# Three edits to an eight-batch attention and MLP kernel: where batch 3's loads are queued, how the ninth chunk's attention is multiplied and evicted, and the order of half-size products

## The chip, the cores and the metric

The kernel runs on one core of a Trainium2 chip. The metric is the device time of one execution in microseconds (us). The engines are named as in the profile: PE is TensorE (matmuls; PEld its weight loads), DVE is VectorE, ACT is ScalarE, POOL is GpSimd, SP is SyncE, which here only issues transfers. Each engine works through its own queue in order. Transfers issued by POOL go into queue q0, those issued by SP into q1.

## The reference

```python
def _attn_ref(q, k, v):                      # (8, 8, 576, 64) each
    q_s = softmax(q over the last axis); k_s = softmax(k over axis 2)
    kv = np.einsum('bhsd,bhse->bhde', k_s, v)
    return np.einsum('bhsd,bhde->bhse', q_s, kv)

def _moe_ref(x, g_ln, w_ch1, w_ch2):         # x: (8, 576, 512), heads side by side
    xn = (x - mean) / sqrt(var + 1e-6) * g_ln
    return x + np.maximum(xn @ w_ch1, 0.0) @ w_ch2     # 512 -> 2048 -> 512
```

The softmax lines are shortened here: the reference subtracts the maximum, and divides by the sum plus 1e-9. All is in float32; the kernel multiplies in bf16 and sums in float32.

## The kernel before

**Chunks.** Each of the 8 batches has 576 rows. The first 512 of each make a chunk (chunk c belongs to batch c), kept as 4 tiles t of 128 rows. The 64 rows left over of all batches are put together as a ninth chunk, C9 = 8: its tile t holds batch 2t in partitions 0 to 63 and batch 2t + 1 in partitions 64 to 127. A chunk passes through attention and then through the MLP, and while PE works on the MLP of chunk c, the attention of chunk c + 1 is slipped in between.

**Attention of a chunk.** ACT takes exp of q (`exp_q`, L193) and k (`exp_k`, L174). A DMA transpose turns exp(q) into `eqT` (`eq_T`, L256). PE forms k·v per pair of heads in `pkv` (`kv_mm`, L308), and DVE writes it, normalised, block-diagonally into `kv_sb` (L318). `po_mm` then multiplies: four matmuls of 128 columns for one tile (L342) into one bank `po`; `x_fast` evicts the bank in one DVE pass (L403) that also multiplies by the reciprocal of the softmax sum and gives the row sum, and `xn_out` (L389) centres the row. `square_sum` (ACT, L377) gives the variance. `xn_T` transposes xn by DMA, two tiles at a time, into `xnT`. `sum_x` (L248) forms four half-size sums `tq` of xnT for the MLP, two instructions each, on POOL for chunks under 8 and on DVE for chunk 8.

In chunk C9 two batches lie in one tile, so `po_mm` multiplies all 128 rows with the kv of both batches (L349, 256 columns, two matmuls in a bank) and half of every result is thrown away: for each pair of matmuls DVE takes the half rows that count in two pieces (L358, 64 partitions x 256). That pass gives no row sum, so `x_rest` takes it on ACT (L418, `AF.Copy` with an accumulator) ahead of `square_sum`.

**MLP of a chunk.** Both matmuls are done with seven half-size products in place of eight (Strassen's scheme in Winograd's form): products 1 to 7 of sums of quarters. In the first matmul (`mm1_fast`, L733) the hidden rows are split in four groups g; groups are taken in pairs (0, 1) and (2, 3). A product of one group is four matmuls of 256 columns. Bank `bx` gets products 1, 6, 7 and 4; ACT copies it after product 1 into `bc` (`seed`, L757), product 5 goes to `bb` and is copied by ACT to `s` (`copy_5`, L761), DVE adds after product 6 (`add_5`, L764: bb = bx + s) and after product 7 (`out_22`, L767, writes hT), and ACT's relus (L779) end the banks. DVE relus what `out_22` wrote for two groups in one instruction (L772). The order that `slot` gives for a pair is: 1, 5 of the first group, 1, 5 of the second; 6, 2 of each; 7, 3 of each; 4 of each.

For the second matmul DVE makes four half-size sums s1 to s4 of the hidden rows, `sum_h(g, i)` (L573), for two halves g of the hidden rows and i = 0 to 3 (s1, s2, s3, s4). `mm2_fast` (L589) takes the products in the order 1, 5, 6, 2, 7, 3, 4, 16 matmuls each, into banks ba, bb, bc, be. Product 5 reads s1, 6 reads s2, 7 reads s3, 3 reads s4. ACT copies ba to s2 and s3 (L614), DVE adds (L617) and makes the output `ot` in quarters (L600), and POOL issues the store (L606). Chunk 8 has its own order (`last_products`: 1, 2, 6, 5, 7, 3, 4) and output tile `yl` (L629). Chunk 0 and the first matmul of chunk 1 use plain matmuls (`ph`, L497, L482; `pc`, L542).

**What sets the order.** Everything is written by hand. `run(main, side)` walks the MLP's steps of one chunk, whose weights add up to a position (one matmul of 256 columns is 0.5, of 512 columns 1); each side step has a position and is issued before the first MLP step at or behind it. `attn_fast` gives the positions of an ordinary chunk's attention, `attn_rest` those of C9, `second_side` those of everything that runs beside chunk 1's MLP, and the list in the call of `run` for chunk 0 those beside chunk 0. `at={7: [...]}` in `mm2_fast` runs steps behind the matmul of that number in a product. In each engine's queue this order is fixed.

**Loads.** `load_batch` clears one element on DVE (L1074) and issues q (L118, 1 MB) or k with its rest (L118, L125) on SP. `load_v` issues v on POOL: for batches 1 and 2 as one transfer into `vt`, copied by `cast_v` (L134), for later ones as four column pieces straight into `vm` (L147) and two of the rest `vr` (L150). `vm` and `vr` have two places, by the batch's parity. In `second_side` q of batch 3 is loaded at position 8, k at 31, `eq_T(2)` stands at 14.2, `load_v(3)` at 12, `load_v(4)` at 60.

**Buffers.** `mm_ps` has six PSUM banks, `att_ps` (pkv, po) two. A new tile waits for the last reader of the bank that it is given.

Of the kernel before, what the change touches and what calls it, by code (L numbers as in the profile page):

```python
# [20 lines left out]
def kernel(  # L21
# [214 lines left out]
    def sum_x(c, i):  # L236
# [9 lines left out]
        eng = nc.gpsimd if c < C9 else nc.vector  # L246
# [88 lines left out]
    def po_mm(c, t, i):  # L335


        if c < B:
            if i == 0:
                pool, tag = (mm_ps, "m") if c == 0 and t >= 2 else (att_ps, "a")  # L340
                pobox["p"] = pobox[c, t] = pool.tile([P, DM], FP32, tag=tag, name="po")
            nc.tensor.matmul(  # L342
                pobox["p"][:, i * P : i * P + P], eqTs[c][:, t, i, :], kv_sb[:, c, i, :],
                start=True, stop=True,
            )
        else:
            if i % 2 == 0:
                pobox[i // 2] = att_ps.tile([P, 2, 2, P], FP32, tag="a", name="po")
            nc.tensor.matmul(  # L349
                pobox[i // 2][:, i % 2], eqTs[c][:, t, i, :],  # L350
                kv_sb[:, 2 * t : 2 * t + 2, i, :], start=True, stop=True,
            )
            if i % 2 == 1:
                hs = slice(2 * i - 2, 2 * i + 2)
                x = xs[c][0][:, t].rearrange("p (h d) -> p h d", h=H)
                for half in range(2):
                    ps = slice(64 * half, 64 * half + 64)
                    nc.vector.tensor_mul(  # L358
                        x[ps, hs, :].rearrange("p (j h) d -> p j h d", h=2),
                        pobox[i // 2][ps, :, half].rearrange("p j (h d) -> p j h d", h=2),  # L360
                        eqs[c][2][ps, t, hs].rearrange("p (j h) -> p j h", h=2).to_broadcast([64, 2, 2, D]),
                    )
# [51 lines left out]

    def x_rest(t):

        x, _, _, mv = xs[C9]
        nc.scalar.activation(  # L418
            scrap, x[:, t], AF.Copy, accum_out=mv[:, t, 0:1]
        )  # L420
        square_sum(C9, t)
# [197 lines left out]
    def last_products(product):  # L619
# [28 lines left out]
        def seed_e():  # L648
# [5 lines left out]
            15: [lambda: both("a", 0, 0), lambda: sum_h(1, 2), lambda: sum_h(1, 3)]})  # L654
        product(2, "c", first=True, at={15: [lambda: both("c", 0, 0, True), lambda: store(0, 2, 0)]})
        product(6, "a", at={15: [lambda: copy_u("s2")]})
# [9 lines left out]
    def mm2_fast(c):  # L666
# [34 lines left out]
        def sums(*which):  # L701
            return [lambda g=g, i=i: sum_h(g, i) for g, i in which if g or c == FAST]

        late, wide = c == FAST, ((1, 2), (1, 3))
        product(1, "a", first=True, cut=6, at={
            0: sums((1, 0), (0, 1), (1, 1)) + ([] if late else sums(*wide[:2 if c < B - 1 else 0])),
            15: [seed_c]})
        product(5, "b", first=True, cut=4, at={
            8: sums((0, 2), (1, 2)) if late else sums(*wide[:1]) if c == B - 1 else []})
        product(6, "a", at={  # L710
            8: sums((0, 3), (1, 3)) if late else sums(*wide[1:]) if c == B - 1 else [], 15: [lambda: copy_u("s2")]})
# [24 lines left out]
    def mm1_fast(c):  # L736
# [37 lines left out]
        def out_relu(g, name, odd, half, eng):  # L774
            dst = h_out(g, odd, half)
            if eng is nc.vector:
                nc.vector.tensor_scalar_max(dst, in0=at[g, name], scalar1=0.0)
            else:
                nc.scalar.activation(dst, at[g, name], AF.Relu)  # L779

        def slot(g, n):
            if n == 0:
                if g == 0:
                    steps.append((0, new_h))
                product(1, g, "x", True, [lambda: seed(g)])
                product(5, g, "b", True, [lambda: copy_5(g)])
            elif n == 1:
                product(6, g, "x", False, [lambda: add_5(g)])
                product(2, g, "c", False, [
                    lambda: out_relu(g, "c", 0, 0, nc.scalar)])  # L790
            elif n == 2:
                product(7, g, "x", False, [lambda: out_22(g)])
                product(3, g, "b", False, [lambda: out_relu(g, "b", 0, 1, nc.scalar)])
            else:
                product(4, g, "x", False, [lambda: out_relu(g, "x", 1, 0, nc.scalar)])

        for g0 in (0, 2):
            for n in range(4):
                for g in (g0, g0 + 1):
                    slot(g, n)  # L800
# [62 lines left out]
    def attn_fast(c):  # L863
# [10 lines left out]
        s += spread([lambda i=i: sum_x(c, i) for i in range(4)], 84, 100)  # L874
        return s

    def second_side():
# [5 lines left out]
        s += [(p, lambda w=w: load_batch(3, (w,))) for p, w in ((8, 2), (31, 0))]  # L883
        s += [(9 + 2 * j, lambda j=j: cast_v(2, j)) for j in range(2)]
        s += [(12, lambda: load_v(3)), (60, lambda: load_v(4))]
# [19 lines left out]
    def attn_rest():  # L905

        s = [(2, lambda: recip_q(C9)), (4, lambda: start_x(C9))]
        for t, (p0, p1, p2, p3) in enumerate(
            ((6, 14, 18, 24), (16, 27, 48, 58), (59, 67, 69, 73), (69, 77, 79, 82))
        ):  # L910
            s += spread([lambda t=t, i=i: po_mm(C9, t, i) for i in range(NP)], p0, p1)
            s += [(p2, lambda t=t: x_rest(t)), (p3, lambda t=t: xn_out(C9, t))]
        s += [(68, lambda: xn_T(C9, 0, 2)), (82.5, lambda: xn_T(C9, 2, 2)), (88, lambda: rstd_op(C9))]
# [278 lines left out]
```

## Time and profile before

| | us |
|---|---|
| median of 3 runs | 284.44 (284.18 to 284.64) |
| the profiled execution | 284.36 |
| its span, first to last instruction | 282.6 |
| PE busy in the span | 269.2 |
| DVE busy | 225.2 |
| ACT busy | 185.6 |
| chunks 3, 4, 5, 6, by their first matmul to the next's | 26.77, 26.77, 26.78, 26.76 |

The page gives each engine's busy time, share of the span and number of instructions; then the span in 40 slices with busy tenths and the granted clock of PE. A PE that is busy is not one at its peak: lengths of matmuls overlap, and a dense run is told by the spacing of starts. Matmul records of 256 columns are 273 ns long and 109 ns apart in a dense run. The waits list who waited for whom, with the total, the number of times and the longest. In a timeline a line is a run of equal instructions: start, length of the run, engine, line, operation, output and inputs, sizes, number, and in brackets how long the engine had stood idle and what ended that. "SPq" is a transfer's issue on SP.

### The profile page before, as it was taken

To read this page: it belongs to the slowest core of one execution; us is meant where nothing else is said; L and a number is where in the kernel's file an instruction comes from. 1 tells how busy PE (TensorE), PEld (TensorE's weight loads), DVE (VectorE), ACT (ScalarE), POOL (GpSimd) and SP (SyncE) were. 2 spreads that over 40 slices of the span, in tenths; PEclk is the share of its full clock that TensorE was granted. 3 is DMA by queue.
4 is the path that set the end of the run, shared out by engine and by line. 5 is a ranking of instruction groups with operands and counts; after the bars stand their busy time and mean duration, and the time that the engine had idled before them with its cause. 6 is when DMAs were issued, how large, how long until landed. Compare 5 with 4: busy or idle time off the path is not lost.

```text
span 282.6 us, 6420 instructions
## 1 busy us (share of the span) xinstructions
PE 269.2 (95%) x2477; PEld 227.3 (80%) x2477; DVE 225.2 (80%) x495; ACT 185.6 (66%) x354; POOL 91.3 (32%) x142
## 2 busy tenths in 40 slices
PE   8999999993999999999999999999999989799994
PEld 5888855771598988998899889898989878688883
DVE  4656795955598899699979997999699898886863
ACT  4547881694397778678858876886788488438600
POOL 3832216356009520781096018003600820011000
PEclk9979999998699999999999999999999999999999
DMA  7999999899968999399849986317803430123014
GB/s 187 243 207 211 332 211 324 190 225 181 200 86 231 266 246 137 87 322 177 150 127 342 84 151 187 129 37 150 259 9 63 87 148 3 37 64 124 2 38 111
DMA packets 85409, 44.99 MB, mean 159 GB/s; under 512 B 62145, under 2 KB 82113, under 8 KB 85378
## 3 DMA queue, kind: packets, MB, share of 16 engines
q0 software_dynamic: 35632, 22.29, 44.1%
q1 hardware_dynamic: 49154, 21.77, 33.5%
q10 hardware_dynamic: 592, 0.52, 0.6%
q8 instruction: 19, 0.31, 0.5%
q14 instruction: 12, 0.10, 0.1%
HBM read 36.70 MB, written 9.44 MB: 163 GB/s over the span
## 4 chain that ended last, share of the span: by engine, by line
PE 81%; DVE 10%; DMA 5%; ACT 1%; issue 1%; DVEq 0%; ACTq 0%
PE ba L589 17%; PE bx L733 16%; PE bb L733 8%; PE ph L497 5%; PE pc L542 4%; PE bb L589 4%; PE be L589 4%; PE bc L589 4%; DMA eqT<-eq 4%; PE bc L733 4%; PE warm L850 4%; PE pkv L308 3%; PE po L342 2%; DVE x L358 2%; PE ph L482 2%; DVE hs L573 2%
## 5 line engine op out<-in xcount | busy, mean ns | idle before, releaser
L589 PEld LDWEIGHTS <-hs 128*128 128x128 bf16 x512 | 49.6, 98 | 7.0 <-issue 1.3
L733 PEld LDWEIGHTS <-w_q 128*128 128x128 bf16 x448 | 41.1, 98 | 5.0 <-issue 0.8
L248 POOL TENSOR_TENSOR tq<-xnT 128x256 bf16<-128x256 bf16 x24 | 15.5, 663 | 91.0 <-DMA xnT<-xn 91.0
L589 PEld LDWEIGHTS <-hT 128*128 128x128 bf16 x384 | 37.2, 98 | 4.4
L733 PEld LDWEIGHTS <-w1g 128*128 128x128 bf16 x336 | 31.3, 98 | 5.9 <-issue 2.1
L733 PE MATMUL bx<-tq,w_q 128*128 128x256 bf16 x224 | 35.1, 273 | 0.2 <-DVE bb L764 0.2
L589 PE MATMUL ba<-w_q,hs 128*128 128x256 bf16 x256 | 31.9, 272 | 1.1 <-ACT s L614 1.1
L764 DVE TENSOR_TENSOR bb<-bx,s 128x512 f32<-128x512 f32 x28 | 19.5, 698 | 12.7 <-ACT s L761 6.6
L757 ACT COPY bc<-bx 128x512 f32<-128x512 f32 x28 | 16.5, 589 | 16.8 <-PE bx L733 16.8
L342 PE MATMUL po<-kv_sb,eqT 128*128 128x128 bf16 x128 | 22.1, 224 | 4.8 <-DMA eqT<-eq 4.6
L403 DVE SCALAR_TENSOR_TENSOR x<-po,rq 128x512 bf16<-128x512 f32 x30 | 20.5, 684 | 6.8 <-PE po L342 6.6
L210 DVE TENSOR_REDUCE zq<-eq 128x16 f32<-128x1024 bf16 (+1 forms) x20 | 20.7, 1050 | 4.9 <-ACT eq L201 2.5
L606 POOL DMA_DIRECT2D out_dram<-ot x28 | 15.3, 553 | 25.8 <-DVE ot L600 25.8
L377 ACT ACTIVATE scrap<-x,mv 128x512 bf16<-128x512 bf16 x32 | 23.1, 721 | 0.6 <-DVE x L403 0.2
L779 ACT ACTIVATE hT<-bc 128x512 bf16<-128x512 f32 x28 | 16.7, 597 | 9.0 <-PE bc L733 8.5
L779 ACT ACTIVATE hT<-bb 128x512 bf16<-128x512 f32 x28 | 16.6, 595 | 9.0 <-PE bb L733 9.0
L573 DVE TENSOR_TENSOR hs<-hT 128x1024 bf16<-128x1024 bf16 x32 | 21.8, 685 | 0.4
L308 PE MATMUL pkv<-vm,ek 128*128 128x130 bf16 x112 | 21.3, 220 | 0.0
L147 POOL DMA_DIRECT2D vm<-in_v_dram x20 | 17.7, 904 | 7.6 <-PE pkv L308 7.1
L767 DVE TENSOR_TENSOR hT<-bx,s 128x512 bf16<-128x512 f32 x28 | 18.6, 687 | 0.8 <-PE bx L733 0.4
L342 PEld LDWEIGHTS <-eqT 128*128 128x128 bf16 x128 | 12.1, 101 | 7.4 <-DMA eqT<-eq 5.1
L733 PE MATMUL bb<-xnT,w_q 128*128 128x256 bf16 x112 | 17.8, 273 | 0.0
(146 smaller groups left out, 610.4 us busy)
## 6 DMA issues: line engine op xcount, KB each, us to landing
out_dram<-ot POOLq DMA_DIRECT2D x32, 256.0 KB, 4.3
qt<-in_q_dram SPq DMA_DIRECT2D x5, 1024.0 KB, 8.7
kt<-in_k_dram SPq DMA_DIRECT2D x5, 1024.0 KB, 8.2
vm<-in_v_dram POOLq DMA_DIRECT2D x20, 128.0 KB, 10.3
w_raw<-in_moe_w_ch_dram POOLq DMA_DIRECT2D x4, 512.0 KB, 12.3
w_sb<-in_moe_w_ch_dram POOLq DMA_DIRECT2D x4, 512.0 KB, 17.7
qt<-in_q_dram POOLq DMA_DIRECT2D x2, 1024.0 KB, 15.5
kt<-in_k_dram POOLq DMA_DIRECT2D x2, 1024.0 KB, 13.7
```

The lines of the kernel that those rows point to most:

```text
L147: nc.gpsimd.dma_start(vm[:, b % 2, t, :, 0:D], src[:, t])
L210: nc.vector.reduce_sum(eqs[c][1][:, ts], eqs[c][0][:, ts], axis=AX.X)
L308: nc.tensor.matmul(pkv[:, j % 2, 0:w], lhsT, rhs, start=(t == 0 and j % 2 == 0), stop=(t == last), skip_group_check=True,)
L342: nc.tensor.matmul(pobox["p"][:, i * P : i * P + P], eqTs[c][:, t, i, :], kv_sb[:, c, i, :], start=True, stop=True,)
L377: nc.scalar.activation(scrap, x[:, t], AF.Square, bias=mv[:, t, 0:1], scale=-float(DM), accum_out=mv[:, t, 1:2],)
L403: nc.vector.scalar_tensor_tensor(x[:, t].rearrange("p (h d) -> p h d", h=H), in0=pobox[c, t].rearrange("p (h d) -> p h d", h=H), scalar=1. ...
L573: nc.vector.tensor_tensor(out=dst, in0=x, in1=y, op=op)
L589: nc.tensor.matmul(hbox[bank][:, t], lhsT, rhs, start=first and (own or t == 0) and k == 0, stop=k == KH - 1, skip_group_check=True)
L733: nc.tensor.matmul(dst[:, q], lhsT, rhs, start=first and q == 0 and ko == 0, stop=ko == 1, skip_group_check=True)
L764: nc.vector.tensor_tensor(out=at[g, "b"], in0=at[g, "x"], in1=at[g, "s"], op=ALU.add)
L767: nc.vector.tensor_tensor(out=h_out(g, 1, 1), in0=at[g, "x"], in1=at[g, "s"], op=ALU.add)
L779: nc.scalar.activation(dst, at[g, name], AF.Relu)
```

## The change

1. **Loads.** In `second_side` q of batch 3 goes from position 8 to 14.3, behind `eq_T(2)`. `load_v(3)` leaves position 12 there and goes to position 109 beside chunk 0's MLP. `load_v(4)` goes from 60 to 90; its place in POOL's queue stays the same, since nothing of POOL's lies between.
2. **Ninth chunk.** `po_mm` for C9 uses two half-row matmuls per pair of heads: 64 columns of weights each, the first half into partitions 0 to 63 of the bank, the second into 64 to 127, each with its own batch's kv, 128 columns. All four pairs of heads go into one bank, and `x_fast` and `square_sum` evict it as in any other chunk. `x_rest` is gone. The positions in `attn_rest` are new.
3. **Products.** `mm1_fast` takes each product for both groups of a pair before the next product: 1, 1, 5, 5, 6, 6, 2, 2, 7, 7, 3, 3, 4, 4. The sums `sum_h` are moved: in chunks 2 to 6 sums s1, s2 and s3 of the first half stand at 30, 33 and 41 (before 33, 36, 39 and 42 for all four), s3 of the second half with s1 and s2 at the start of the second matmul, and both halves of s4 behind half of product 6. In chunk 7 s3 and s4 of both halves are moved behind half of products 5 and 6, in chunk 8 behind products 2 and 6.
4. **Sums of xn.** In `attn_fast` the four `sum_x` stand at 84, 88, 92, 101 (before 84, 88, 92, 96); of chunk 7 the second of them is on DVE, at 100.

```diff
@@ sum_x
-        eng = nc.gpsimd if c < C9 else nc.vector
+        eng = nc.vector if c == C9 or (c == C9 - 1 and i == 1) else nc.gpsimd
@@ po_mm
+        if i == 0:
+            pool, tag = (mm_ps, "m") if c == 0 and t >= 2 else (att_ps, "a")
+            pobox["p"] = pobox[c, t] = pool.tile([P, DM], FP32, tag=tag, name="po")
...
         else:
-            if i % 2 == 0:
-                pobox[i // 2] = att_ps.tile([P, 2, 2, P], FP32, tag="a", name="po")
-            nc.tensor.matmul(
-                pobox[i // 2][:, i % 2], eqTs[c][:, t, i, :],
-                kv_sb[:, 2 * t : 2 * t + 2, i, :], start=True, stop=True,
-            )
-            if i % 2 == 1:
...
-                for half in range(2):
-                    ps = slice(64 * half, 64 * half + 64)
-                    nc.vector.tensor_mul(
...
+            for half in range(2):
+                ps = slice(64 * half, 64 * half + 64)
+                nc.tensor.matmul(
+                    pobox["p"][ps, i * P : i * P + P], eqTs[c][:, t, i, ps],
+                    kv_sb[:, 2 * t + half, i, :], start=True, stop=True,
+                )
@@ x_rest
-        nc.scalar.activation(
-            scrap, x[:, t], AF.Copy, accum_out=mv[:, t, 0:1]
-        )
-        square_sum(C9, t)
@@ last_products
-            15: [lambda: both("a", 0, 0), lambda: sum_h(1, 2), lambda: sum_h(1, 3)]})
-        product(2, "c", first=True, at={15: [lambda: both("c", 0, 0, True), lambda: store(0, 2, 0)]})
-        product(6, "a", at={15: [lambda: copy_u("s2")]})
+            15: [lambda: both("a", 0, 0)]})
+        product(2, "c", first=True, at={7: [lambda g=g: sum_h(g, 2) for g in range(2)],
+            15: [lambda: both("c", 0, 0, True), lambda: store(0, 2, 0)]})
+        product(6, "a", at={7: [lambda g=g: sum_h(g, 3) for g in range(2)], 15: [lambda: copy_u("s2")]})
@@ mm2_fast
-            return [lambda g=g, i=i: sum_h(g, i) for g, i in which if g or c == FAST]
+            return [lambda g=g, i=i: sum_h(g, i) for g, i in which if g or c == FAST or i == 3 or c == B - 1 and i > 1]
...
-            0: sums((1, 0), (0, 1), (1, 1)) + ([] if late else sums(*wide[:2 if c < B - 1 else 0])),
+            0: sums((1, 0), (0, 1), (1, 1)) + ([] if late else sums((1, 2))),
...
+            8: sums((0, 3), (1, 3)), 15: [lambda: copy_u("s2")]})
@@ mm1_fast
-        for g0 in (0, 2):
-            for n in range(4):
-                for g in (g0, g0 + 1):
-                    slot(g, n)
+        for g0 in (0, 2):
+            for n, name, first, after in plan:
+                for g in (g0, g0 + 1):
+                    product(n, g, name, first, [lambda g=g, after=after: after(g)])
@@ attn_fast
-        s += spread([lambda i=i: sum_x(c, i) for i in range(4)], 84, 100)
+        s += [((84, 100 if c == C9 - 1 else 88, 92, 101)[i], lambda i=i: sum_x(c, i)) for i in range(4)]
@@ second_side
-        s += [(p, lambda w=w: load_batch(3, (w,))) for p, w in ((8, 2), (31, 0))]
+        s += [(p, lambda w=w: load_batch(3, (w,))) for p, w in ((14.3, 2), (31, 0))]
-        s += [(12, lambda: load_v(3)), (60, lambda: load_v(4))]
+        s += [(90, lambda: load_v(4))]
@@ attn_rest
-            ((6, 14, 18, 24), (16, 27, 48, 58), (59, 67, 69, 73), (69, 77, 79, 82))
+        for t, (p0, p1, p2) in enumerate(((6, 22, 46), (40, 54, 62), (59, 66, 69), (68, 75, 77))):
             s += spread([lambda t=t, i=i: po_mm(C9, t, i) for i in range(NP)], p0, p1)
-            s += [(p2, lambda t=t: x_rest(t)), (p3, lambda t=t: xn_out(C9, t))]
+            s += [(p1, lambda t=t: x_fast(C9, t)), (p2, lambda t=t: square_sum(C9, t))]
@@ beside chunk 0
+            + [(109.0, lambda: load_v(3)), (128.0, lambda: xn_pT(1, 2, nc.scalar))]
@@ the calls of run
-            sums = [(57, 0)] if c == FAST else [(p, i) for i, p in enumerate((30, 50, 53, 55) if c == B - 1 else (33, 36, 39, 42))]
+            sums = [(57, 0)] if c == FAST else [(p, i) for i, p in enumerate((30, 41) if c == B - 1 else (30, 33, 41))]
...
-        run(mlp_steps(C9), [(33 + 3 * i, lambda i=i: sum_h(0, i)) for i in range(4)])
+        run(mlp_steps(C9), [(33 + 3 * i, lambda i=i: sum_h(0, i)) for i in range(2)])
```

`plan` lists the products with their banks and the step that follows each: 1 (x, `seed`), 5 (b, `copy_5`), 6 (x, `add_5`), 2 (c, relu), 7 (x, `out_22`), 3 (b, relu), 4 (x, relu).

## The prediction

> **What bounds the kernel now.** First the engine table and clock row of the page, then what TensorE (PE) waited for, then the stretches by stage, last the timeline around each wait. In the page, the shares and the granted clock in 40 slices of 7.07 us:
>
> ```profile
> PE 269.2 (95%) x2477; PEld 227.3 (80%) x2477; DVE 225.2 (80%) x495; ACT 185.6 (66%) x354; POOL 91.3 (32%) x142
> ...
> PEclk9979999998699999999999999999999999999999
> ```
>
> PE is the bound, so the change can pay only where PE stands still or runs at a lower clock. PE's waits (us in total, times, longest):
>
> ```profile
> PE po L342 <- DMA eqT<-eq: 4.6, 1, 4.6
> PE ba L589 <- ACT s L614: 1.1, 1, 1.1
> ...
> PE po L349 <- DVE x L358: 0.8, 1, 0.8
> PE bx L733 <- DVE hT L767: 0.7, 2, 0.5
> ```
>
> One wait is large, and the clock's dip (the tenth and eleventh slice, 63.6 to 77.7) sits on it. The timeline there (start, length):
>
> ```profile
> 56.38 0.39 SPq L118 DMA_DIRECT2D qt<-in_q_dram  x1
> ...
> 59.27 5.78 SPq L256 DMA_TRANSPOSE eqT<-eq  x1
> ...
> 70.76 0.29 PE L342 MATMUL po<-kv_sb,eqT 128*128 128x128 bf16 x1 [4.57 <-DMA eqT<-eq]
> ...
> 71.48 0.63 PE L482 MATMUL ph<-xnT,w1g 128*128 128x512 bf16 x1
> ```
>
> Batch 2's transpose is issued 2.9 us behind batch 3's q load on the same queue. Its issue takes 5.78 us where the seven have a median of 1.86, and it lands after 11.4 us where the median is 4.4. After the wait 512-wide matmuls come 0.43 apart instead of 0.215, until 75.3.
>
> In steady chunk 5 and in chunk 7, which carries the ninth chunk's attention (busy us per engine, then clock, DMA share, GB/s):
>
> ```profile
> 169.90:196.68 26.78, 26.78 (x263) 23.98 (x261) 23.55 (x50) 20.39 (x38) 7.17 (x13) 1.00 0.48 126
> ...
> 223.44:254.50 31.06, 28.24 (x254) 24.42 (x252) 26.56 (x59) 19.61 (x44) 5.30 (x11) 1.00 0.20 60
> ```
>
> A steady chunk is dense. Chunk 7 is not, and DVE is its fullest other engine.
>
> **A, batch 3's loads.** On SP the transpose now precedes the q load; batch 3's v load (six POOL issues) goes ahead of batch 0's four stores. The transpose then has no load ahead of it on its queue. In q0 the v load runs beside it: its last column piece takes the semaphore of batch 2's v load (44.4 + 8.5 = 52.9), so issue ends near 55 and data near 64. A half-size transpose beside such a v load (76.7) landed in 3.9 us where the median is 3.3; so 4.4 x 3.9/3.3 = 5.2, landing 64.5. Batch 2's kv_sb is ready at 66.3 and becomes what is late, just where PE arrives (66.2).
>
> From 66.35 PE has, up to chunk 2's first product, 15 matmuls of 512 columns x 0.215 = 3.22, 112 of 256 x 0.109 = 12.23 and 16 of 128 x 0.055 = 0.88 (spacings of dense runs): it ends at 82.7, where before it ended at 89.34. That is 6.65. DVE loses the cover of the stall: summing its queue from 67.67 by steady spacings (x and xn 1.0 each, a half-sum 0.61, a reduction 1.13, eight ot pieces 0.39 each) puts the last ot near 84.6; the fourth product group of chunk 2, at 84.15, takes that bank. So 0.55 comes back: **-6.1**, bounds -6.8 and 0.
>
> Behind the moved waits: q, k, ktr of batch 3 and both xn transposes on SP. q goes out at 61.1; with 7.0 (this load before) it lands at 68, with 11.6 (the slowest later one) at 72.7, exactly where ACT wants it. POOL's stores start near 55 instead of 52.4; their buffers are next needed near 80. POOL's earlier issues lie beside DVE copies; one such copy took 0.87 instead of 0.41 (56.22). The xn at 49.1 could slip 0.46; its transpose on PE has 0.67 of slack. Cost 0, bounds 0 and 0.5. The load of batch 4 keeps its place on POOL.
>
> **B, product order and half-sums, chunks 2 to 6.** In the timeline of chunk 5:
>
> ```profile
> 180.65 0.69 DVE L764 TENSOR_TENSOR bb<-bx,s 128x512 f32<-128x512 f32 x1
> 181.25 0.68 DVE L573 TENSOR_TENSOR hs<-hT,hs 128x1024 bf16<-128x1024 bf16 x1
> 181.85 1.28 DVE L767 TENSOR_TENSOR hT<-bx,s 128x512 bf16<-128x512 f32 x2
> ...
> 182.59 1.19 PE L733 MATMUL bx<-tq,w1g 128*128 128x256 bf16 x8
> ```
>
> The po before these eight started at 182.39, so 0.145 is lost; the product 1 behind them starts at 183.62 instead of 183.46: 0.16. PE waits here for the L767 pair, which stands behind a fourth half-sum. The change moves that half-sum behind x_fast, into the second matmul. In the new order each bank is still touched again 12 matmuls (1.31) later; the tightest step is the second L764 of a pair: ready 0.27 after its product, queued 0.17 behind the first, 0.70 long, so 1.14 of 1.31. The two late half-sums end near 20.4 us into the chunk, their product starts at 23.0. 5 x 0.30 = **-1.5**, bounds -1.5 and +2.0 (both L764 0.2 late in each chunk).
>
> **C, the ninth chunk's attention.** Out: 16 DVE pieces at 0.42 and four ACT sums at 0.63 + 0.19. In: four DVE passes at 0.68 + 0.08, and 32 half-row matmuls for 16. PE's four waits in chunk 7 (0.24, 0.52, 0.75, 1.11, each with 0.16 of drain: 273 ns long, 109 apart) make 3.27; chunk 7 takes 252.83 - 223.28 = 29.55 for 240 x 0.109 = 26.2. By the new DVE queue all four go: the last pass ends 18.8 us in, ACT's s2 copy at 20.4, its reader at 21.0. One tq sum moves from POOL to DVE at the end of chunk 6; it waits for POOL's first sum (23.8) when DVE gets there at 24.1, and the ot pieces behind it end 0.3 late for chunk 7's fourth group: +0.3.
>
> The half-row matmuls (128 rows by 64 columns of the array) have no row here. If one costs a 128-column po, 32 x 0.055 equals 16 x 0.109: nothing added. But the array's shape changes 32 times, in and out of 16 pairs. Only near two rows does the shape change before:
>
> ```profile
> 10.97 0.27 PE L850 MATMUL warm<-junk 128*128 128x256 bf16 x1
> 11.17 0.69 PE L1013 MATMUL gps<-g_row,ones_f 1*128 1x512 f32 x1
> ...
> 12.83 0.24 PE L1017 MATMUL gcp<-ones_f,g_row 1*128 1x1 f32 x1
> 13.01 0.33 PE L285 MATMUL z<-ones,ek 96*128 96x1 bf16 x7
> ```
>
> They start 0.09 and 0.08 later than the spacing before (0.109 and 0.10). From below a change costs 0; from above, a whole 273 ns matmul and a bare 98 ns weight load: 0.371, or 11.9 for 32. I take 0.085, the nearest rows: 2.7. Together -3.3 + 0.3 + 2.7 = **-0.3**, bounds -3.0 and +8.9.
>
> The Trainium skill speaks against this step: TensorEngine Tiling (Array Packing), Key Properties, says that a change of the tiling mode, not merely of the tile, drains the array. If that is the 0.164 between a matmul's length and its spacing, my estimate by that page is 32 x 0.164 = 5.2 and the whole 278.1; the two rows above show about half.
>
> **D, chunk 8.** 253.70 x4 should end at 254.14, the next group starts at 254.50 (waiting for ot): 0.36. Before and behind its last L733 groups 0.04, 0.32 and 0.16 are lost as in B. The ot backlog goes with DVE's relief, the rest with the moved half-sums: **-0.9**, bounds -0.9 and 0.
>
> **Sum.** -6.1 - 1.5 - 0.3 - 0.9 = -8.8. The profiled execution took 284.36 (span 282.6 and 1.8 around it): 275.6. The median of the three runs, 284.44, is 0.08 above it: within rounding of 275.6 too.
>
> **Rivals.**
> 1. Shape changes are free: 2.7 less, 272.9. For it: po rows ride at 0.055 among wider matmuls without a gap. Against: those rows don't change the shape. 0.25.
> 2. The transpose stays late: v load, stores and the transpose still fill the 16 engines and it lands near 70.7. A = 0: 281.7. For: in stretches of 2 us the DMA share is 0.5 to 0.85 from 52 to 60 and up to 2.25 behind. Against: the 3.9 us landing beside the v load at 76.7. 0.10.
> 3. Slower: in chunk 7 every shape change drains PE and loads weights bare, 0.371: 11.9 for 2.7, so 284.36 - 8.8 + 9.2 = 284.8. It decides from (8.8 + 2.7)/32 = 0.36 per change. Against: 0.08 and 0.09. 0.06.
> 4. Between, about 0.2 per change: 279.3. 0.14.
>
> The forecast has 0.45. The range reaches from 272.2 (A at -6.8, C at -3.0, B and D whole) to 280.0; outside lie rivals 2 and 3, 0.16. About 0.2% (0.6 us) is what a measurement of this kernel can tell from no change. Faster 0.92, same 0.02, slower 0.06, from these cases.
>
> **What would show it.** A: eqT<-eq lands in 4.4 to 6 us, no 0.5 clock after 60, chunk 2 starts near 82.7 to 83.5. B: steady chunks of 26.45 to 26.5. C: a chunk 7 of 29.2 (26.2 with free changes, over 35 in rival 3), with the gaps at the 64-column groups. D: chunk 8 without a wait on ot. The forecast is wrong if q of batch 3 lands after 72.7 and ACT stops before s2, or if a DVE wait replaces the removed one in chunk 2.

## The result, and the profile after

The changed kernel took 275.44 us in the median of 4 executions (272.78 to 278.09), the kernel before 284.47 beside it (284.18 to 284.64); the ratio is 0.9607, 95% interval 0.9575 to 0.9638. That ratio leaves out executions more than 1.5% above the fastest of their kernel, which here takes out the changed kernel's own two at 277 and 278; the medians of all differ by 9.0 us. The forecast was 275.6. The times after are spread over 5.3 us, those before over 0.5, and this spread turned out to be the key.

The profiled execution after took 278.09, with a span of 276.3. From the page, the engine table and the clock row (40 slices of 6.9 us):

```profile
PE 266.7 (97%) x2490; PEld 224.4 (81%) x2493; DVE 219.8 (80%) x489; ACT 179.1 (65%) x346; POOL 90.5 (33%) x140
...
PEclk9999999997799999999999999999999999999999
```

The dip after 60 is still there. What PE waited for (us in total, times, longest):

```profile
PE po L342 <- DMA eqT<-eq: 3.7, 1, 3.7
PE warm L820 <- DVE junk L944: 1.1, 1, 1.1
PE ptr L892 <- DVE xn L386: 0.2, 1, 0.2
```

The waits of chunks 2 to 8 (on s, x, hT) are gone; the wait for batch 2's transpose has stayed. Steady chunk 5 and all of chunk 7 (busy us per engine, clock, DMA share, GB/s):

```profile
165.77:192.25 26.48, 26.48 (x262) 23.95 (x261) 23.39 (x50) 19.82 (x38) 7.30 (x13) 1.00 0.48 127
218.73:247.71 28.98, 28.98 (x258) 22.35 (x257) 21.84 (x50) 15.82 (x33) 3.35 (x7) 1.00 0.19 56
```

PE is busy throughout both, and DVE in chunk 7 has 21.84 us of work, where the whole of that chunk held 25.07 before. Around the transpose (start, length; "SPq" and POOL's DMA rows are issues):

```profile
55.93 2.24 POOL L501 DMA_DIRECT2D out_dram<-ot  x4
...
56.53 5.07 SPq L256 DMA_TRANSPOSE eqT<-eq  x1
...
61.71 0.88 SPq L118 DMA_DIRECT2D qt<-in_q_dram  x1
...
67.16 0.29 PE L342 MATMUL po<-kv_sb,eqT 128*128 128x128 bf16 x1 [3.70 <-DMA eqT<-eq]
...
67.24 0.63 PE L464 MATMUL ph<-xnT,w1g 128*128 128x512 bf16 x1
```

The q load is behind the transpose now, and yet the transpose lands 10.58 us after its issue (11.45 before). Batch 0's four output stores are issued just ahead of it. After the wait the clock's record shows half speed from 65.74 to 72.57.

Where the 6.25 us between the two spans (282.56 and 276.31) come from, by the starts of the same matmuls:

| stretch | before | after | difference | forecast |
|---|---|---|---|---|
| to chunk 1's first matmul | 53.84 | 51.10 | -2.74 | 0 |
| from there to chunk 2's first product ("the stretch") | 35.50 | 35.07 | -0.43 | -6.65 |
| chunk 2 | 26.86 | 26.48 | -0.38 | -0.30 + 0.55 |
| chunks 3 to 6, each | 26.77 | 26.48 | -0.29 | -0.30 |
| chunk 7 | 29.55 | 28.98 | -0.57 | -0.3 |
| chunk 8, to the last matmul's start | 25.28 | 24.34 | -0.94 | -0.9 |

The small rest lies behind the last matmul. Everything behind chunk 2's start came about as forecast (the 0.55 in chunk 2 was part of A's price and stayed away with it). Part A did not come in this execution; a beginning that the change does not touch gave 2.74 in its place. So the questions were: why is the transpose still late, what is the beginning, and what are parts B and C made of.

### The profile page after: what moved, and what is told of

It is laid out like the page before. It is cut to its first block, busy times and chain, and to the rows that moved or that the text cites. A ratio compares the mean times of both kernels' runs of the same rounds, so it can differ in the third digit from the quotient of the medians.

```text
span 276.3 us, 6429 instructions
## 1 busy us (share of the span) xinstructions
PE 266.7 (97%) x2490; PEld 224.4 (81%) x2493; DVE 219.8 (80%) x489; ACT 179.1 (65%) x346; POOL 90.5 (33%) x140
## 4 chain that ended last, share of the span: by engine, by line
PE 90%; DMA 4%; DVE 3%; ACT 1%; issue 0%; DVEq 0%
PE ba L571 20%; PE bx L716 18%; PE bb L716 9%; PE bb L571 5%; PE bc L571 5%; PE be L571 5%; PE ph L479 5%; PE bc L716 5%; PE pc L524 4%; DMA eqT<-eq 4%; PE warm L820 3%; PE pkv L308 3%; PE po L342 3%; PE ph L464 2%; PE ptr L892 1%; PE po L349 1%
## 5 line engine op out<-in xcount | busy, mean ns | idle before, releaser
L248 POOL TENSOR_TENSOR tq<-xnT 128x256 bf16<-128x256 bf16 x24 | 15.8, 677 | 88.8 <-DMA xnT<-xn 88.8
L716 PEld LDWEIGHTS <-w_q 128*128 128x128 bf16 x448 | 40.3, 98 | 4.4
L393 DVE SCALAR_TENSOR_TENSOR x<-po,rq 128x512 bf16<-128x512 f32 x34 | 23.3, 686 | 9.9 <-PE po L342 7.4
L716 PE MATMUL bx<-tq,w_q 128*128 128x256 bf16 x224 | 31.0, 273 | 0.0
L747 DVE TENSOR_TENSOR bb<-bx,s 128x512 f32<-128x512 f32 x28 | 18.3, 695 | 12.7 <-ACT s L744 11.5
L740 ACT COPY bc<-bx 128x512 f32<-128x512 f32 x28 | 15.0, 582 | 16.8 <-PE bx L716 16.8
L758 ACT ACTIVATE hT<-bc 128x512 bf16<-128x512 f32 x28 | 15.7, 596 | 11.1 <-PE bc L716 10.9
L758 ACT ACTIVATE hT<-bb 128x512 bf16<-128x512 f32 x28 | 15.6, 596 | 10.7 <-PE bb L716 10.6
L308 PE MATMUL pkv<-vm,ek 128*128 128x130 bf16 x112 | 21.3, 220 | 0.0
L571 PE MATMUL bb<-w_q,hs 128*128 128x256 bf16 x128 | 17.1, 273 | 0.0
```

Source lines behind the costliest of these rows:

```text
L308: nc.tensor.matmul(pkv[:, j % 2, 0:w], lhsT, rhs, start=(t == 0 and j % 2 == 0), stop=(t == last), skip_group_check=True,)
L393: nc.vector.scalar_tensor_tensor(x[:, t].rearrange("p (h d) -> p h d", h=H), in0=pobox[c, t].rearrange("p (h d) -> p h d", h=H), scalar=1. ...
L571: nc.tensor.matmul(hbox[bank][:, t], lhsT, rhs, start=first and (own or t == 0) and k == 0, stop=k == KH - 1, skip_group_check=True)
L716: nc.tensor.matmul(dst[:, q], lhsT, rhs, start=first and q == 0 and ko == 0, stop=ko == 1, skip_group_check=True)
L747: nc.vector.tensor_tensor(out=at[g, "b"], in0=at[g, "x"], in1=at[g, "s"], op=ALU.add)
L758: nc.scalar.activation(h_out(g, odd, half), at[g, name], AF.Relu)
```

## The experiments

Theory at first: batch 3's early v load is what the transpose shares the 16 DMA engines with. Rival: it is late beside any load, wherever v stands. Kernels are compared by the landing (issue to landing of batch 2's transpose), the stretch, and the times. "Before" in this section is the kernel before, run beside each on the same chip.

**before_again** and **after_again**: both kernels unchanged.

> The kernel before, unchanged, for another look at its beginning. In the first trace of the changed kernel the part ahead of chunk 1 (which the change does not touch) ends 2.74 us earlier than in the first trace of the kernel before: chunk 1's first matmul starts at 51.10, not 53.84. Theory: the beginning varies from execution to execution by up to about 2.7 us with the clock that PE is granted there, and the kernel before hides this, since PE then waits for the transpose of exp(q) of batch 2 anyway. Then all times stay within 284.0 to 284.9, whatever their mean clock. Rival: the beginning is always the long one here, and the change shortens it by some side effect: chunk 1's first matmul at 53.8 again and the same mean clock of 0.982 in every run.

> The changed kernel, unchanged, for more times and another trace. In its first trace the transpose of exp(q) of batch 2 landed 10.58 us after its issue and PE waited 3.70 us for it, with half clock from 65.74 to 72.57; yet its times run from 272.78 to 278.09. Theory: an execution loses up to 3.7 + 3.4 us here, or nothing, according to how its beginning stands against the landing of batch 3's v load; times from 271 to 278.5 with a spread of over 3 us, and where the trace shows a landing under 7 us it shows no 0.5 clock after 60. Rival: the wait is there in each execution and only the beginning (2.74 us) differs: spread of at most 3 us, the wait over 3 us again.

Measured: before 283.61 (281.91 to 286.08, 12 executions), chunk 1's first matmul at 51.36, landing 11.66, stretch 35.66, span 280.28. After 276.42 (272.92 to 278.41, 6), 51.53, landing 9.94, wait 3.1, stretch 33.46; half clock for only 3.41 us (66.98 to 70.39). Half of the theory for the kernel before falls: the beginning does vary there as well, but it is not hidden; its times carry it. For the changed kernel the spread of 5.5 goes with the theory and not with the rival; an execution that loses nothing was not traced. The transpose is issued 2.5 us earlier with a short beginning, and lands earlier by 2.3. On this chip the medians differ by 282.99 - 276.42 = 6.6 us (ratio, counted as in the result, 0.9691, 0.9627 to 0.9754).

**v_back**: the v load at its old place, the q load behind the transpose. **loads_back**: both at their old places.

```diff
@@ second_side (v_back)
-        s += [(90, lambda: load_v(4))]
+        s += [(12, lambda: load_v(3)), (90, lambda: load_v(4))]
@@ list beside chunk 0 (v_back)
-            + [(109.0, lambda: load_v(3)), (128.0, ...)]
+            + [(128.0, ...)]
@@ second_side (loads_back has this too)
-        s += [... for p, w in ((14.3, 2), (31, 0))]
+        s += [... for p, w in ((8, 2), (31, 0))]
```

> The changed kernel with batch 3's v load back at its old place beside chunk 1 (behind batch 0's four stores); the q load stays behind the transpose. Theory: the early v load's small packets (1.5-us windows of q0 with a busy share of 2.2 to 4.5 between 51.5 and 58) are what the transpose has to share the engines with; without them it lands in 4.4 to 6 us, PE waits under 1 us, there is no 0.5 clock after 60, and the time is 270.5 to 273.5 in nearly every run, at least 2 us under the changed kernel's median. Rival: the v load is in the way at either place (in the kernel before its packets ran from 62 to 69 beside the transpose): landing over 9 us, wait over 2 us, time 275 to 279, no better than the changed kernel.

> The changed kernel with both loads of batch 3 back at their old places: parts 2 to 4 of the change alone. All theories: PE waits over 4 us for the transpose again, with half clock after it, whatever the beginning. From the first traces the rest is worth 1.54 (chunks 2 to 6), 0.57 (chunk 7) and 0.94 (chunk 8), 3.05 in all: 281.4, within 281.0 to 282.0, with a spread under 0.7. If it is over 283, the rest was worth less than the two traces say; under 280, the loads were worth less.

Measured: v_back 277.93 (276.32 to 278.59), landing 10.79, wait 3.9, stretch 35.16. The rival is right: moving the v load back does not free the transpose. loads_back 281.22 (279.59 to 283.75), landing 12.24, stretch 36.20; steady chunks 26.48, chunk 7 28.98. So parts 2 to 4 give 282.99 - 281.22 = 1.8 by medians (ratio 0.9944, 0.9909 to 0.9979), the q load's move 3.3 more, and the v load's move 1.5 more: part A is worth 4.8 by medians. The time fits the expectation, the spread (4.2, not under 0.7) does not. Nor does the gain on this chip, 1.8 by medians where 3.05 was expected: the traces of before_again and loads_back do show 2.97 less in chunks 2 to 8, but a stretch that is 0.54 longer takes back a part.

What runs beside the transpose differs between v_back and the changed kernel. In v_back from 59 to 67 (queue: packets, MB, share of the 16 engines' time; packets overlap in the record, so a share can pass 100%):

```profile
q0 software_dynamic: 2725, 0.34, 87.7%
q1 hardware_dynamic: 2476, 0.93, 79.9%
```

In the changed kernel from 59 to 65:

```profile
q1 hardware_dynamic: 2096, 0.57, 74.0%
q0 software_dynamic: 202, 0.65, 44.1%
```

In v_back it is many small packets (0.34 MB in 2725): batch 3's v, and from 63 on batch 4's, whose issue follows on POOL at 62.32. In the changed kernel it is few large ones (0.65 MB in 202): batch 0's stores. In v_back POOL issues them from 49.77 to 53.68, as they become ready; in the changed kernel its queue holds them behind the moved v load, and they go out at 55.93. So the theory was put more widely: whatever runs in q0 then.

**v_gated**: nothing may run in q0 beside the transpose. A small POOL copy that reads eqT stands ahead of both v loads.

```diff
@@ second_side (load_v(3) is taken out of the list beside chunk 0)
-        s += [(90, lambda: load_v(4))]
+        s += [(15, lambda: nc.gpsimd.tensor_copy(out=gate, in_=eqTs[2][:, 0, 0, 0:4]))]
+        s += [(15.1, lambda: load_v(3)), (90, lambda: load_v(4))]
```

> The changed kernel with batch 3's v load, and with it batch 4's, held back on POOL until the transpose of exp(q) of batch 2 has landed (one small POOL copy that reads eqT stands ahead of them). In the traces so far q0 was never quiet beside that transpose: with the v load moved forward its packets and batch 0's four stores, with it at the old place its packets and those of batch 4's v load; the landing took 9.9 to 12.2 us in all five, and from chunk 1's first matmul to chunk 2's first product 35.50, 35.66 (before), 35.07, 33.46 (changed), 35.16 (v load back). Theory (whatever runs in q0 shares the engines with the transpose): with q0 quiet the landing takes 4.3 to 6 us, PE waits under 0.5 us, no 0.5 clock after 60, that stretch is 29 to 30, and the time is 269 to 272.5. Rival (the transpose is slow there for a reason of its own, such as its place behind the issue of the clearing instructions or the q load behind it on its queue): landing over 9 us and a stretch over 33 again, time 275 to 279. A third: the landing is early but batch 3's v comes too late for chunk 2, PE waits for it there, and chunk 2 takes over 27.

Measured: landing 4.43, no wait, no half clock there, stretch 28.67 after a beginning of 51.37. The wide theory is right about the landing. But the time is 275.65 (273.8 to 277.4) and not under 272.5; in the trace chunk 2 takes 30.26, as in the third case, though PE waits there not for v but for a sum of xn:

```profile
PE bb L716 <- POOL tq L248: 2.0, 1, 2.0
```

Both v loads now run beside the transposes of xn, the sums of xn come late, and the clock halves again (83.71, 3.41 us). The jam had only been moved.

**old_sums** and **old_order**, meant for part B:

```diff
@@ mm1_fast (old_order: products per group, as before)
-            for n, name, first, after in plan:
+            for part in (plan[:2], plan[2:4], plan[4:6], plan[6:]):
                 for g in (g0, g0 + 1):
-                    product(n, g, name, first, ...)
+                    for n, name, first, after in part:
+                        product(n, g, name, first, ...)
@@ old_sums: positions of sum_h in run(), mm2_fast and last_products as in the kernel before
```

> The changed kernel with the half-size products of the first matmul in the old order (1, 5 of the first group, 1, 5 of the second, and so on), the half-sums at their new places. Theory (the gain of 0.29 in each steady chunk comes from the half-sum that was moved into the second matmul): steady chunks stay at 26.45 to 26.55. Rival (it comes from the order): they go back to 26.75 to 26.80. Between the two, 26.6 to 26.7, each has a part.

> The changed kernel with the half-sums back at their old places, the half-size products in the new order. Theory (the half-sums alone): steady chunks go back to 26.75 to 26.80, and chunk 8 from its first product to the last matmul's start from 24.34 to 24.8. Rival (the order): steady chunks stay at 26.45 to 26.55 and chunk 8 at 24.34.

Measured, one execution of each (old_order 276.94, old_sums 278.15): old_order has steady chunks of 26.48, the same as the changed kernel; in chunks 3 to 6 the order of the products is worth nothing by itself. old_sums has 26.95, worse than before (26.77) and than either case expected; chunk 8 takes 24.87 (expected 24.8), chunk 7 29.40. PE there waits, once in each of chunks 2 to 6 and once in chunk 8:

```profile
PE bx L715 <- DVE bb L746: 1.9, 6, 0.3
```

So the gain is the half-sums', and with these at their old places the new order costs 0.18 a chunk (together with part 4 of the change, which old_sums keeps and which was not tried alone). By chance old_sums' trace was also the first of a changed kernel with the long beginning (53.49). There the v load is through (its last column piece landed at 59.25) and little of the stores is left when the transpose's packets start to move, past 60:

```profile
55.88 2.70 POOL L501 DMA_DIRECT2D out_dram<-ot  x4
58.93 3.25 SPq L256 DMA_TRANSPOSE eqT<-eq  x1
62.28 0.52 SPq L118 DMA_DIRECT2D qt<-in_q_dram  x1
```

It lands after 5.66, and the stretch is 28.56. The stores are issued at the same 55.9 as in the changed kernel, behind the last piece of the v load, which comes at 53.79 and 53.67, nearly the same with either beginning; the transpose comes 2.4 later. From 60.5 to 64.5:

```profile
q1 hardware_dynamic: 2183, 0.63, 107.7%
q0 software_dynamic: 26, 0.05, 3.5%
```

**late_begin**: the same with added work, so that it isn't chance.

```diff
@@ first_batch
         warm(6)
-        warm(6)
+        warm(28)
```

> The changed kernel with 22 more warming matmuls ahead of chunk 0 (28 in place of 6 in the last such run), about 22 x 0.109 = 2.4 us of work that computes nothing. The traces show two beginnings: chunk 1's first matmul near 51.3 (seven traces) or near 53.7 (two). With the early v load and the short beginning the transpose is issued near 56.8, shares the engines with batch 0's four stores and lands after 9.9 to 10.9; with the long one (old_sums: issue 58.93) the v packets and the stores are done when it starts, it lands after 5.66, and from chunk 1's first matmul to chunk 2's first product it takes 28.56 instead of 33.3 to 35.3. Theory (what decides is when PE and ACT come to the transpose against the end of q0's loads): the added 2.4 us make the short beginning into the long one, landing 4.5 to 6.5 us, no wait over 1 us, no 0.5 clock after 60, stretch 28.4 to 29.5, and the time falls in spite of the added work: 271.5 to 274.5 in most runs, median at least 1.5 under the 276.4 of the changed kernel. Rival (the long beginning and the early landing met by chance): the work is added to everything, 277.5 to 280.

Measured: in the traced execution chunk 1 starts at 53.50, the landing is 5.48, the stretch 28.55, no wait for eqT and no half clock before the end; span 273.0, 3.3 less than the changed kernel's first trace, with 2.4 us of useless work in it. The traced landing and time (274.78) fit the theory. The median does not: 276.88 (274.56 to 277.09), no better than the changed kernel's 276.42, where at least 1.5 less was expected. Four of six lie near 277, 2.2 above the traced one, which would fit the long beginning with the added work on top (their mean granted clock is 0.990 to 0.994, the traced one's 0.998); none of those was traced.

**grouped**: all eight half-row matmuls of a tile in one run.

```diff
@@ po_mm, ninth chunk
-            for half in range(2):
-                ps = ...
-                nc.tensor.matmul(pobox["p"][ps, i * P : i * P + P], ...)
+            for j in range(NP if i == NP - 1 else 0):
+                for half in range(2):
+                    ps = ...
+                    nc.tensor.matmul(pobox["p"][ps, j * P : j * P + P], ...)
```

> The changed kernel with the eight half-row matmuls of one tile of the ninth chunk in one run, in place of four pairs among the other matmuls: the array's shape changes 8 times and not 32. In the changed kernel's trace a pair costs 0.272 beyond the matmuls around it (0.202 from the wide matmul's start to the pair, the two 0.003 apart, 0.176 to the next wide one, less 0.109). Theory (the price is per change of shape): a run of four pairs costs 0.093 + 3 x 0.055 + 0.176 = 0.43 in place of 1.09, chunk 7 becomes 28.98 - 2.6 = 26.4, bounds 26.2 and 26.9. Rival (the price lies in the half-row matmul itself, whatever stands beside it): chunk 7 stays at 28.7 to 29.1. The time goes with it, but its spread is wider than this gain.

Measured: chunk 7 takes 26.29, 2.69 less. In the changed kernel a pair breaks a dense run like this:

```profile
219.44 0.60 PE L716 MATMUL bb<-tq,w_q 128*128 128x256 bf16 x4
219.97 0.25 PE L349 MATMUL po<-kv_sb,eqT 128*64 128x128 bf16 x2
220.15 0.61 PE L716 MATMUL bb<-tq,w_q 128*128 128x256 bf16 x4
```

From the fourth wide matmul to the pair it is 0.202 (dense: 0.109), the two of the pair start 0.003 apart, and from the second to the next wide one it is 0.176. So a pair adds 0.272 to the dense spacing. In grouped all eight add 0.44:

```profile
222.54 0.60 PE L717 MATMUL bx<-tq,w_q 128*128 128x256 bf16 x4
223.07 0.41 PE L350 MATMUL po<-kv_sb,eqT 128*64 128x128 bf16 x8
223.41 0.61 PE L717 MATMUL bx<-tq,w_q 128*128 128x256 bf16 x4
```

The price is per change of shape. The time is 273.08 (272.02 to 275.90; ratio 0.9609, 0.9562 to 0.9656), though the traced execution (275.90) still has the late transpose: short beginning, landing 10.87.

**store_gate** (grouped, the stores held back until the transpose has landed, v 4 behind the sums of xn) and **v_gate_late4** (grouped, v 3 held back as in v_gated, v 4 behind the sums of xn):

```diff
@@ y_out (store_gate)
-            eng.dma_start(out..., ot)
+            held.append(lambda: eng.dma_start(out..., ot))
@@ second_side (store_gate)
-        s += [(90, lambda: load_v(4))]
+        s += [(15, lambda: nc.gpsimd.tensor_copy(out=gate, in_=eqTs[2][:, 0, 0, 0:4]))]
+        s += [(15.1, lambda: [go() for go in held]), (109, lambda: load_v(4))]
@@ second_side (v_gate_late4, against v_gated)
-        ... (90, lambda: load_v(4))]
+        ... (109, lambda: load_v(4))]
```

> The grouped kernel with batch 0's four stores, not batch 3's v load, held back on POOL until the transpose of exp(q) of batch 2 has landed, and batch 4's v load issued behind the sums of chunk 2's xn (position 109). The v load keeps its early place. Theory: q0 is quiet from 58 on whatever the beginning; the transpose lands in 4.3 to 6.5 us, no wait over 1 us, the stretch from chunk 1's first matmul to chunk 2's first product is 28.3 to 29.5, chunk 2 takes 26.5 to 27.4 (no wait for tq as in v_gated, since no v packets lie beside the transposes of xn), chunk 7 26.3. The time is 268.5 to 271.5 with the short beginning and up to 2.5 more with the long one. Rival: something else comes late in their place (ot buffers of chunk 1 that wait for the held stores, or batch 4's v for chunk 3): chunk 1, 2 or 3 takes over 1.5 us more, and the time is 272 or more.

> v_gated with the ninth chunk's matmuls grouped and batch 4's v load issued behind the sums of chunk 2's xn (position 109). In v_gated the stretch was 28.67, but chunk 2 took 30.26: PE waited 1.96 us for tq and had half clock from 83.71 for 3.41 us, and the two transposes of xn and the next one of exp(q) (issue 6.15 us long, landing 8.60) lay beside both v loads. Theory (batch 4's v packets made those late): stretch 28.5 to 29, chunk 2 26.5 to 27.5, time 268.5 to 271.5 with the short beginning. Rival (batch 3's v packets alone do it): chunk 2 over 29 again, time 271.5 to 274.

Measured: store_gate: landing 4.42, stretch 28.56 (beginning 53.58), chunk 2 27.25, but chunk 3 33.14, time 276.75 (276.0 to 279.3); the rival holds, in a form that it did not name. Batch 4's v load, issued from 83.75 on, has landed by 100.9, ahead of the transposes of chunk 3's xn (100.15 and 105.91) and of exp(q) of batch 4 (101.58). But batch 5's v load, behind it on POOL, goes out from 100.05 on (from 87.09 in stores_sp below), right beside them; they land after 6.42, 7.91 and 11.44, and PE waits:

```profile
PE bb L718 <- POOL tq L248: 4.8, 1, 4.8
```

v_gate_late4: landing 4.41, stretch 28.55, chunk 2 27.30, chunk 3 28.23 with 1.4 of the same wait, 274.38 (271.83 to 276.85). In v_gated chunk 2's loss was batch 4's v then, as expected, but at 109 it costs chunk 3 1.75, again with batch 5's v (from 93.34 to 100.3) beside the first transpose of chunk 3's xn, which lands after 7.38. The traced execution, 271.83 with a beginning of 51.41, is 0.3 above the range given for the short beginning; the median is far above it.

**stores_sp**: grouped, and the four stores issued by SP, ahead of the transpose, in place of POOL.

```diff
@@ y_out
-        eng = eng or nc.gpsimd
+        eng = nc.sync
```

> The grouped kernel with batch 0's four stores issued by SP ahead of the transpose, not by POOL behind batch 3's v load; nothing is held back. In the changed kernel those stores (256 KB each) run from 57.5 to 65 in q0, beside the transpose, only because they queue behind the v load; they are ready at 50 to 54. Theory (the stores are what the transpose shares the engines with; the v packets end at 58 whatever the beginning): they go out between 50 and 57 beside the v packets, the transpose lands in 4.5 to 7 us with either beginning, no wait over 1 us, no 0.5 clock after 60, the stretch is 28.5 to 30, chunk 2 takes 26.5 to 27.4, chunks 3 to 6 26.48 each and chunk 7 26.3: 269.5 to 271 with the short beginning, 271.5 to 273.5 with the long one, median 1 to 3 under grouped (273.08). Rival (a transfer ahead of the transpose on its own queue delays it, as the q load did before): landing over 8 us again, stretch over 32, time 273 to 276.

Measured: 272.06 (270.96 to 273.37; ratio 0.963, 0.9583 to 0.9677, beside 282.82). PE waits nowhere for eqT with a short beginning (51.59); the stretch is 28.56, chunk 2 27.25, chunks 3 to 6 26.48. From its page and its timeline:

```profile
PE 262.3 (97%) x2493; PEld 223.7 (83%) x2493; DVE 220.3 (82%) x489; ACT 178.9 (66%) x346; POOL 88.4 (33%) x136
...
PEclk9999999999999999999999999999999999999999
```

```profile
49.91 3.30 SPq L502 DMA_DIRECT2D out_dram<-ot  x4
...
57.03 4.23 SPq L256 DMA_TRANSPOSE eqT<-eq  x1
```

The stores leave at 49.91 in place of 55.93. The v load still runs beside the transpose (its last column piece lands at 61.34), so here it is the stores that made it late. The trace holds no landing for this transpose; that it comes in time is read from PE, which doesn't wait for it. The six times fall into two groups, 270.96 to 271.15 and 272.97 to 273.37: what is left of the spread is about the size of the two beginnings' difference, and the mean granted clock goes with it (0.998 in the first group, 0.990 and 0.991 in the second). It beats both kernels. Chunk 7 took 27.25 here and not 26.29: two subtractions on DVE (L248, a sum of xn) took 1.44 together where grouped has 0.48, and the outputs behind them were late. In every trace of a kernel with part 4 POOL runs a subtraction of its own (L248) beside this pair. Here and in old_sums (where the pair took 1.42, and the late outputs are 0.36 of its longer chunk 7) POOL's had begun 0.05 and 0.07 before the pair. In the other ten it began at most 0.04 before; there the pair took 0.48, and POOL's one took 1.0 in place of 0.66. So one of the two engines is held up each time. That the order of their starts decides which was not tried.

## Why the prediction was right, and where it was not

The number was right: 275.6 against a median of 275.44, with 276.42 on a second chip. By the traces three of four terms were right in mechanism and nearly in size. Part A was right for one of two beginnings only; by medians it gave 4.8 where 6.1 was said. That the number fits so closely is luck: in the profiled execution A gave 0.43, and a short beginning, which the prediction didn't count, gave 2.74 in its place; four times between 272.78 and 278.09 then had their median near the forecast. On the second chip the medians differ by 6.6 and not by 8.8.

**A, -6.1.** The working started from the beginning of the profile before, 53.84. With that beginning its times hold almost to the letter: in old_sums and late_begin the transpose lands after 5.66 and 5.48 (5.2 was said), chunk 2 starts at 82.05 (82.7), the stretch is 6.9 shorter (6.65), and 0.78 comes back in chunk 2 by the late ot (0.55; 27.26 against 26.48 in late_begin). The picture behind the 5.2 does not hold: it has the v load beside the transpose until 64, but there the load had landed at 59.25, and q0 moved 26 packets from 60.5 on. With the short beginning, which ten of the fourteen traces have and which the prediction didn't know of, the four traces that have all of part A and a late transpose (after, after_again, grouped, old_order) show landings of 9.9 to 10.9 and stretches of 33.3 to 35.3, where before_again has 35.66: a gain of 0.3 to 2.3 only. Rival 2 (the transpose stays late beside the v load and the stores, given 0.10) is what the profiled execution shows; its time is under that rival's 281.7 because its beginning was 2.74 shorter.

The step that failed: "POOL's stores start near 55 instead of 52.4; their buffers are next needed near 80", at a cost of 0. The stores did start at 55.9. The prediction looked at who needs their buffers and not at what their 1 MB does beside the transpose; its comparison, a half-size transpose that landed in 3.9 "beside such a v load" (76.7), had no stores beside it, and hardly the v load either: in the trace of before 22 of its packets moved up to 78, while q0 was still full, and 1034 from 78 to 81, when q0 moved none. stores_sp, which differs from grouped only in when and where they are issued, gives the short beginning a stretch of 28.56 too.

Why two engines' queues slow each other: the trace has both busy on the same 16 engines (74.0% and 44.1%). The Trainium skill, DMA: Bandwidth & Descriptors, Queues, rings and completion order, says that each DMA engine takes turns between the queues that have work for it, one packet at a time. The rows are consistent with that, since both queues move packets in the same window, but they show neither the turns nor whether the profile's packets are the page's. By it few large packets could take as much as many small ones; that it is the packets' size that counts was not tried.

What stays open: some executions of the changed kernel (272.78 and 272.92) are too fast for a long beginning with an early landing (late_begin's sum, 274.78), and must have had the short one with an early landing; their mean granted clock of 1.000, where the traced late landings went with 0.988 to 0.994, says the same. None of them was traced, so what lets the transpose through in them is not known.

**B, -1.5.** Steady chunks 26.48, said 26.45 to 26.5; chunks 2 to 6 gave 1.54. old_order and old_sums, one trace of each, show that it is the half-sums, as the prediction argued. That the order is neutral holds only with the new sums.

**C, -0.3.** Chunk 7 gave -0.57 and took 28.98 where 29.2 was said. All four waits went. A pair adds 0.272 to the dense spacing; less 0.109 for the matmul that it replaces this is 0.163 x 16 = 2.6, said 2.7. It is made up differently: the changes of shape cost 0.093 going in and 0.121 (0.176 less the 0.055 of a 128-column matmul) coming out, 0.214 a pair where 0.17 was taken; and the two half-row matmuls take the time of one, where two were counted. So 2.7 is nearly right because these two errors nearly cancel. The 0.3 for late ot pieces came only in old_sums and stores_sp. Rivals 1, 3 and 4 are out. The two rows that the price was taken from were not the only ones: at 15.84 in the profile before, at half clock, the matmuls go from 96 rows of the array to 128 with no gap at all (0.106, the spacing before it too), so not every change of shape has a price. The prediction's estimate that took the drain of the Trainium skill's page TensorEngine Tiling (Array Packing), Key Properties, to be 0.164 per change (5.2 for 32 changes) was too high: 16 x 0.214 = 3.4.

**D, -0.9.** Measured -0.94. As said, it has two parts: in old_sums the wait for ot at the start of chunk 8 is gone too, but with the half-sums at their old places 0.53 is lost there (24.87 for 24.34), most of it at one wait for DVE's `add_5`.

## What to carry to other kernels

A load moved forward in a queue pushes back what stood behind it there: ask not only who needs those buffers but what their traffic will run beside, above all a transfer that PE waits for. Where one execution's beginning differs from another's by microseconds, work through a race between transfers and compute for both; one profile shows one of them. Matmuls of another shape were cheapest in one run here, since the price lay in going in and out.

## What the runs showed of the hardware that was not expected

- **The beginning has two lengths.** In ten traces 15 to 21 of the first 43 spacings of warming matmuls were of half clock, and chunk 1 started at 51.1 to 51.6 (late_begin had 21 and, with its 2.4 added, started at 53.5). In three (before, old_sums, store_gate) it was 25 to 28, half clock came back for 3.41 us at 13.3 to 13.9, where the 24 matmuls of L308 took over 2.5 in place of 1.5, and chunk 1 started at 53.5 to 53.8. Full clock was first granted at 4.3 to 5.5 us with a short beginning (late_begin too) and at 6.4 to 7.0 with a long one. Half clock after full came, ahead of the last matmuls, only in stretches of 3.41 or 6.83 us. The Trainium skill, TensorE: Matmul & The Clock Gate, Part 1, has a free-running window of 3413 ns and a cold start that varies from run to run. The traces agree: the stretches are one and two such windows.
- **Two half-row matmuls in the two column halves of the array start 0.003 us apart** and take the time of one (in grouped the later pairs of a run start 0.056 apart, a single 128-column matmul takes 0.055).
- **A wait costs twice.** The waits for eqT of 3.0 and 3.1 us brought 3.41 us at half clock, those of 3.7 to 5.4 brought 6.83. Length alone does not decide: those for tq, of 2.0 (v_gated) and 4.8 (store_gate), brought 3.41 each.
